# One substitution run for units 0 and 1, an unprepared unit 0, wider small matmuls and a new order in a deltanet and low-rank-mixer kernel

## The chip, the cores and the metric

The kernel runs on one core of a Trainium2 chip. A core has a matmul engine (PE, with its own weight loads, PEld), a vector engine (DVE), a scalar engine (ACT), a general engine (POOL), a queue engine (SP) and DMA queues. Each engine takes its instructions in the order in which they were written for it; semaphores hold an instruction back until what it reads is there. The metric is the device time of one execution in microseconds (us).

## The reference

Two blocks follow each other. The first is a delta-rule recurrence over 768 steps, for 4 batches x 8 heads of width 48; the second mixes tokens with a rank-32 product and then runs a two-layer channel MLP.

```python
k_n = k / (norm(k) + 1e-06)
for t in range(768):
    y[:, :, t] = q_t @ state                      # 48 x 48 state per head
    v_old = state^T k_t
    state = state + beta_t * outer(k_t, v_t - v_old)

x = y as (4, 768, 384)
u = x + ((x^T @ U) @ V)^T                         # U 768 x 32, V 32 x 768
out = u + relu(u @ w_ch1) @ w_ch2                 # 384 -> 1536 -> 384
```

## The kernel before

The recurrence is computed in chunks of 64 tokens. Within a chunk the steps form a unit lower triangular system, whose inverse (with beta and the norms in it) is called Z here. With it a chunk needs only matmuls: `z = Z v - (Z k) s`, `y = q s + (masked q k) z`, `s = s + k z`, where s is the state. Six chunks of all 8 heads of one batch make a unit; there are 8 units (2 for each batch, `units[n]`), which live in turn in two big tiles (`slots`). For a unit n the steps are:

- `load`: DMAs of k, q, v, and of `z` (a second copy of half of k with its token halves swapped, in `kz`), issued on SP, ACT and POOL.
- `grams`: PE transposes of k and q (`turn`, L672), copies by ACT (`placed`), then the products k k^T and q k^T (`products`, L700), of which DVE lays the 32-wide diagonal blocks into `diag` (L713) and masks the q k^T part (L731, one instruction for each half).
- `norms`: ACT root, then a chain of small DVE instructions to the scale `cp`, which is also copied onto the diagonal of `xt` (L627).
- `blocks`: DVE transposes the diagonal blocks into `gs` (L794), scales them (L798) and substitutes: for 31 columns, or 15 where a unit's 32-blocks are halved (units 0, 1 and 2), one product (L803) and one subtraction (L809) each. L816 transposes the result back into `zz`.
- `joins`: matmuls that put together 16-blocks into 32-blocks and these into 64-blocks. For units 0 and 1 (`lone`) the first two stages work on 64 x 64 tiles of the array with 16 moving columns (L860 and L874, 48 profile rows for each stage and half of a unit), the later ones on 32 x 32 tiles (L900 to L921).
- `prepare`: Z is multiplied into k (L1023) and v (L1034) for the whole unit, half by half.
- `recur` and `outputs`: for each chunk the matmuls on the state, L1072 (`b`), L1100 (the new state), L983 and L997 (the two parts of y), 16 rows each, with the DVE instructions L1085 (z) and L1111 (s) between them.

When all 12 chunks of a batch have their y in X, `front` does the token mixing (L1393, L1412, L1436) and `wide` the MLP in three blocks of 256 tokens (`channels` L1497, `narrow` L1617). The next batch's units run beside the MLP of the batch before. Ahead of the first `front` there is nothing of this kind: the head of the kernel holds units 0 and 1, all of batch 0's recurrence and, on ACT and DVE, the conversion of the 64-bit weights (`load_weights`: L1198 on ACT, L1212, L1219 and L1226 on DVE). Its raw data are staged in rooms of other tiles, two of them in w2_sb.

PSUM banks are handed out by the kernel in pairs. The order of everything is written out by hand: `ORDER` numbers some 2260 steps, and each engine receives its instructions in that order. So a step that waits holds all later steps of its engine.

The time lines below name the scalar engine's sequencer and the others' with a "q" (SPq). fp32 matmuls show as two rows each, transposes as one.

Of the kernel before, what the change touches and what calls it, by code (L numbers as in the profile page):

```python
# [27 lines left out]
def kernel(  # L28
# [114 lines left out]

    ORDER = """
    add_up b0 i0 f00: 590 628 635; add_up b0 i0 f03: 659 670 676; add_up b0 i1 f00: 795 820 825; add_up b0 i1 f03:
    840 846 849; add_up b0 i2 f00: 954 1014 1042; add_up b0 i2 f03: 1030 1053 1058; add_up b1 i0 f00: 1146 1147 1163;
    add_up b1 i0 f03: 1186 1188 1192; add_up b1 i1 f00: 1313 1315 1347; add_up b1 i1 f03: 1363 1364 1371; add_up b1
    i2 f00: 1482 1490 1493; add_up b1 i2 f03: 1543 1551 1561; add_up b2 i0 f00: 1688 1689 1692; add_up b2 i0 f03:
    1708 1721 1727; add_up b2 i1 f00: 1844 1845 1846; add_up b2 i1 f03: 1888 1889 1892; add_up b2 i2 f00: 2027 2051
    2056; add_up b2 i2 f03: 2046 2047 2053; add_up b3 i0 f00: 2183 2184 2189; add_up b3 i0 f03: 2187 2188 2190;  # L150
    add_up b3 i1 f00: 2205 2206 2208; add_up b3 i1 f03: 2203 2204 2207; add_up b3 i2 f00: 2226 2229 2230; add_up b3
    i2 f03: 2227 2228 2231; blocks n0: 67 71 72 73 76 78 79 80 84 85 88 95 100 101 102 106 107 109; blocks n1: 134
    151 155 160 162 169 192 196 200 208 209 212 220 222 226 232 233 235; blocks n2: 482 491 495 498 500 502 508 510
    511 513 516 519 521 522 528 529 530 537; blocks n3: 700 718 722 724 727 732 733 753 757 761 766 768 769 770 772
    774 778 784 787 791 792 798 799 811 812 814 815 819 824 831 847 848 851 854; blocks n4: 966 976 978 979 982 986
    988 997 1006 1020 1028 1029 1038 1048 1063 1072 1078 1082 1084 1094 1096 1106 1107 1108 1109 1111 1112 1113 1117
    1118 1121 1123 1125 1132; blocks n5: 1175 1190 1207 1210 1217 1219 1223 1224 1235 1236 1239 1246 1254 1258 1270
    1275 1279 1284 1285 1286 1290 1291 1294 1295 1298 1301 1302 1323 1324 1328 1331 1335 1336 1342; blocks n6: 1507
    1519 1531 1533 1542 1552 1559 1565 1570 1572 1574 1578 1579 1588 1591 1599 1606 1616 1628 1639 1640 1644 1645
    1649 1650 1654 1656 1660 1661 1663 1665 1667 1669 1677; blocks n7: 1670 1729 1732 1735 1742 1746 1754 1762 1768  # L160
    1776 1781 1782 1795 1797 1799 1805 1806 1810 1830 1832 1833 1835 1839 1847 1852 1857 1865 1868 1869 1871 1872
    1887 1890 1894; both f0: 2123; both f1: 2141; both f2: 2143; both f3: 2121; both f4: 2176; both f5: 2191;
    channels b0 i0 e0: 541 542; channels b0 i0 e1: 543 545; channels b0 i0 e2: 546 548; channels b0 i0 e3: 575 579;
    channels b0 i0 e4: 594 595; channels b0 i0 e5: 608 620; channels b0 i1 e0: 764 775; channels b0 i1 e1: 777 781;
    channels b0 i1 e2: 783 785; channels b0 i1 e3: 793 802; channels b0 i1 e4: 804 805; channels b0 i1 e5: 816 833;
    channels b0 i2 e0: 897 898; channels b0 i2 e1: 909 911; channels b0 i2 e2: 912 934; channels b0 i2 e3: 945 963;
    channels b0 i2 e4: 964 965; channels b0 i2 e5: 969 1002; channels b1 i0 e0: 1122 1137; channels b1 i0 e1: 1139
    1140; channels b1 i0 e2: 1141 1142; channels b1 i0 e3: 1145 1148; channels b1 i0 e4: 1149 1165; channels b1 i0
    e5: 1166 1167; channels b1 i1 e0: 1272 1304; channels b1 i1 e1: 1305 1307; channels b1 i1 e2: 1309 1310; channels
    b1 i1 e3: 1312 1314; channels b1 i1 e4: 1316 1333; channels b1 i1 e5: 1334 1350; channels b1 i2 e0: 1440 1441;  # L170
    channels b1 i2 e1: 1447 1449; channels b1 i2 e2: 1463 1464; channels b1 i2 e3: 1466 1499; channels b1 i2 e4: 1501
    1514; channels b1 i2 e5: 1515 1528; channels b2 i0 e0: 1668 1671; channels b2 i0 e1: 1672 1673; channels b2 i0
    e2: 1682 1684; channels b2 i0 e3: 1685 1686; channels b2 i0 e4: 1690 1699; channels b2 i0 e5: 1700 1701; channels
    b2 i1 e0: 1804 1808; channels b2 i1 e1: 1809 1812; channels b2 i1 e2: 1815 1827; channels b2 i1 e3: 1855 1858;
    channels b2 i1 e4: 1860 1861; channels b2 i1 e5: 1875 1877; channels b2 i2 e0: 1951 1961; channels b2 i2 e1: 1963
    1964; channels b2 i2 e2: 1966 1977; channels b2 i2 e3: 1984 1992; channels b2 i2 e4: 2002 2012; channels b2 i2
    e5: 2024 2034; copies f0: 2081 2091; copies f1: 2131 2135; copies f2: 2083 2092; copies f3: 2085 2109; copies f4:
    2155 2156; copies f5: 2149 2162; cut f0 k0 to0: 2116; cut f0 k0 to1: 2126; cut f0 k1 to1: 2114; cut f1 k0 to0:
    2144; cut f1 k0 to1: 2173; cut f1 k1 to1: 2178; cut f2 k0 to0: 2106; cut f2 k0 to1: 2172; cut f2 k1 to1: 2137;
    cut f3 k0 to0: 2134; cut f3 k0 to1: 2122; cut f3 k1 to1: 2138; cut f4 k0 to0: 2160; cut f4 k0 to1: 2177; cut f4  # L180
    k1 to1: 2193; cut f5 k0 to0: 2166; cut f5 k0 to1: 2192; cut f5 k1 to1: 2186; diagonals n0 h0: 189 190 191 213 214
    224; diagonals n0 h1: 167 168 172 178 181 194; diagonals n1 h0: 302 306 311 319 334 346; diagonals n1 h1: 286 297
    316 317 320 321; diagonals n2 h0: 572 573 574 588 593 611; diagonals n2 h1: 615 632 660 692 701 704; diagonals n3
    h0: 865 866 881 883 884 888; diagonals n3 h1: 858 859 860 861 869 900; diagonals n4 h0: 1161 1174 1203 1204 1213
    1216; diagonals n4 h1: 1155 1156 1157 1160 1195 1209; diagonals n5 h0: 1354 1362 1387 1392 1394 1396; diagonals
    n5 h1: 1359 1360 1365 1395 1405 1406; diagonals n6 h0: 1723 1726 1736 1758 1767 1772; diagonals n6 h1: 1710 1711
    1752 1785 1786 1792; diagonals n7 h0: 1900 1901 1903 1906 1909 1912; diagonals n7 h1: 1904 1910 1920 1927 1933
    1935; first f0: 2097; first f1: 2133; first f2: 2105; first f3: 2103; first f4: 2159; first f5: 2165; front b0
    i0: 487 496 504 505 526 535; front b0 i1: 556 567 607 625; front b0 i2: 626 639 662 671; front b1 i0: 1047 1057
    1066 1079 1101 1105; front b1 i1: 1225 1234 1241 1250; front b1 i2: 1344 1349 1404 1426; front b2 i0: 1576 1592  # L190
# [416 lines left out]

    def landed(name, n, j=1):
        return need(*[(name, n, g, j) for g in range(2)])

    def norms(n):

        _, _, _, _, _, vn, _, _ = units[n]
# [1082 lines left out]
```

## Time and profile before

| | us |
|---|---|
| median of 3 runs | 597.41 |
| lowest and highest run | 595.88, 597.56 |
| the profiled execution's own time | 596.68 |
| its span, first to last instruction | 595.0 |
| PE busy | 560.1 (94%) |
| DVE busy | 409.8 (69%) |
| ACT busy, POOL busy | 217.0, 133.3 |
| first matmul of unit 0's joins (L860) | at 32.0 |
| first matmul of the recurrence (L997) | at 57.7 |
| unit 1's `prepare` (L1034) begins | at 84.25 |
| last matmul of batch 0's recurrence ends | at 107.4 |
| first matmul of the MLP (L1497) | at 116.0 |

The profile's first part gives busy time by engine, the second the span in 40 slices of 14.9 us with busy tenths, the granted PE clock (PEclk, tenths of full speed) and DMA use. A group line reads "line engine operation out<-in shapes xcount | busy, mean ns | idle before". A line of a window table gives the stretch, its length, each engine's busy time with its number of rows, the granted clock, the DMA share and GB/s. Timeline rows give start, duration, engine, line and shapes. PE busy near 100% does not say that PE is at full speed: the clock row has to be read with it.

### The profile page before, as it was taken

To read this page: it belongs to the slowest core of one execution; us is meant where nothing else is said; L and a number is where in the kernel's file an instruction comes from. 1 tells how busy PE (TensorE), PEld (TensorE's weight loads), DVE (VectorE), ACT (ScalarE), POOL (GpSimd) and SP (SyncE) were. 2 spreads that over 40 slices of the span, in tenths; PEclk is the share of its full clock that TensorE was granted. 3 is DMA by queue.
4 is the path that set the end of the run, shared out by engine and by line. 5 is a ranking of instruction groups with operands and counts; after the bars stand their busy time and mean duration, and the time that the engine had idled before them with its cause. 6 is when DMAs were issued, how large, how long until landed. Compare 5 with 4: busy or idle time off the path is not lost.

```text
span 595.0 us, 23442 instructions
## 1 busy us (share of the span) xinstructions
PE 560.1 (94%) x10428; PEld 482.4 (81%) x10428; DVE 409.8 (69%) x1011; ACT 217.0 (36%) x442; POOL 133.3 (22%) x229
## 2 busy tenths in 40 slices
PE   4797987899999999999999999999999999999997
PEld 4696876688989987989889888898899778556997
DVE  3889767899999359999893389998973154122542
ACT  2558374436313442144234340234343321334000
POOL 8142133215041507312105143250110000000000
PEclk9657556999999999999999999999999999999999
DMA  9762656624041225510302035420201000000000
GB/s 141 152 154 72 216 116 146 140 70 70 3 95 22 46 42 91 99 47 17 75 2 41 11 54 93 105 58 15 68 6 37 3 2 15 26 0 1 26 28 28
DMA packets 89445, 36.23 MB, mean 61 GB/s; under 512 B 75456, under 2 KB 87104, under 8 KB 89344
## 3 DMA queue, kind: packets, MB, share of 16 engines
q1 hardware_dynamic: 80800, 24.69, 19.4%
q0 software_dynamic: 6944, 9.74, 8.2%
q8 instruction: 82, 1.34, 1.0%
q10 hardware_dynamic: 1600, 0.30, 0.3%
q14 instruction: 19, 0.16, 0.1%
HBM read 29.98 MB, written 4.72 MB: 58 GB/s over the span
## 4 chain that ended last, share of the span: by engine, by line
PE 90%; DVE 4%; issue 2%; ACT 2%; DMA 1%; SPq 0%; DVEq 0%; ACTq 0%
PE P L1617 29%; PE P L1497 25%; PE P L1296 7%; PE P L700 4%; PE P L1072 3%; PE P L983 2%; PE P L997 2%; PE P L672 2%; PE P L874 2%; PE P L1100 2%; PE P L1034 2%; PE P L1023 2%; PE P L860 2%; PE P L1412 2%; PE P L1436 1%
## 5 line engine op out<-in xcount | busy, mean ns | idle before, releaser
L1497 PE MATMUL P<-ut,w_sb 128*128 128x256 f32 x648 | 150.3, 385 | 0.9 <-ACT ut L1439 0.9
L1497 PEld LDWEIGHTS P<-ut,w_sb 128*128 128x128 f32 x648 | 119.8, 190 | 17.8 <-ACT ut L1439 1.1
L1617 PE MATMUL P<-w_sb,hs 128*128 128x192 f32 x540 | 95.8, 330 | 0.0
L1617 PEld LDWEIGHTS P<-w_sb,hs 128*128 128x128 f32 x540 | 87.4, 190 | 3.6 <-issue 1.8
L809 DVE TENSOR_TENSOR xt<-xt,prod 128x112 f32<-128x112 f32 (+21 forms) x200 | 64.6, 323 | 6.9
L803 DVE TENSOR_TENSOR prod<-gs,xt 128x112 f32<-128x112 f32 (+21 forms) x200 | 63.5, 318 | 3.6
L1537 DVE TENSOR_TENSOR X<-X,P 128x192 f32<-128x192 f32 x84 | 29.0, 348 | 49.6 <-PE P L1617 49.4
L1462 ACT ACTIVATE hs<-P 128x512 f32<-128x512 f32 x54 | 32.3, 598 | 80.0 <-PE P L1497 70.4
L967 ACT COPY X<-P 64x192 f32<-64x192 f32 x96 | 30.1, 313 | 60.7 <-PE P L997 59.6
L1617 PE MATMUL P<-w_sb,S 128*128 128x192 f32 x288 | 50.6, 330 | 0.0
L1617 PEld LDWEIGHTS P<-w_sb,S 128*128 128x128 f32 x288 | 46.6, 190 | 1.6 <-issue 1.2
L939 ACT COPY slot<-zz 32x384 f32<-32x384 f32 x64 | 32.2, 508 | 17.2 <-DVE zz L816 10.5
L555 POOL DMA_DIRECT2D slot<-in_v_dram x32 | 21.2, 665 | 66.9 <-DVE slot L747 33.4
L700 PE MATMUL P<-slot 48*64 48x64 f32 x1536 | 32.0, 235 | 4.4 <-ACT slot L687 3.7
L700 PEld LDWEIGHTS P<-slot 48*64 48x64 f32 x1536 | 28.9, 148 | 8.7 <-ACT slot L687 5.0
L1085 DVE TENSOR_TENSOR z<-slot,P 128x192 f32<-128x192 f32 x44 | 15.4, 350 | 29.2 <-PE P L1072 28.9
L946 POOL MEMSET slot<- 32x384 f32 x32 | 13.2, 413 | 96.0 <-PE P L900 52.2
L1296 PE MATMUL P<-slot,w_sb 128*128 128x384 f32 x96 | 33.2, 487 | 0.6 <-ACT slot L1365 0.6
L541 POOL DMA_DIRECT2D slot<-in_q_dram x40 | 24.6, 621 | 40.8 <-DVE slot L747 28.1
L541 POOL DMA_DIRECT2D slot<-in_k_dram x40 | 24.5, 620 | 35.5 <-DVE prod L803 18.6
L555 POOL DMA_DIRECT2D slot<-in_k_dram x44 | 29.5, 675 | 9.0 <-PE P L1100 8.7
L1305 DVE TENSOR_TENSOR slot<-slot,P 128x384 f32<-128x384 f32 x18 | 9.3, 551 | 32.4 <-PE P L1296 24.3
(153 smaller groups left out, 926.0 us busy)
## 6 DMA issues: line engine op xcount, KB each, us to landing
out_dram<-X SPq DMA_DIRECT2D x22, 192.0 KB, 2.6
w_sb<-in_moe_w_ch_dram SPq DMA_DIRECT2D x10, 384.0 KB, 5.2
slot<-in_k_dram SPq DMA_DIRECT2D x48, 72.0 KB, 3.4
slot<-in_k_dram POOLq DMA_DIRECT2D x44, 72.0 KB, 3.3
slot<-in_v_dram SPq DMA_DIRECT2D x32, 72.0 KB, 3.4
slot<-in_v_dram POOLq DMA_DIRECT2D x32, 72.0 KB, 3.6
X<-in_moe_w_ch_dram SPq DMA_DIRECT2D x6, 384.0 KB, 4.4
wide<-in_moe_w_ch_dram SPq DMA_DIRECT2D x6, 384.0 KB, 4.7
```

What stands on the lines that cost most here:

```text
L541: queue.dma_start(out=blocked(n)[quarter(y % 4), j, g, :, 0:w], in_=src[b, 4 * g + 2 * j + par, hf * UC * L : (hf + 1) * UC * L, BK * low ...
L555: queue.dma_start(out=t[half(1 - g if name == "z" else g), :, to, 0:D], in_=src[b, 4 * g + s, hf * UC * L : (hf + 1) * UC * L, :].rearrang ...
L700: nc.tensor.matmul(p_g[half(g ^ (par * i)), par, c], kq[rows, c, j, 0, half(g)], kq[rows, c, j, i, half(g)], start=True, stop=True,)
L803: nc.vector.tensor_tensor(out=prod, in0=gb[:, :, j : j + 1, j + 1 :].to_broadcast([128, split, m, w]), in1=xb[:, :, 0:m, j : j + 1].to_bro ...
L809: nc.vector.tensor_tensor(out=xb[:, :, 0:m, j + 1 :], in0=xb[:, :, 0:m, j + 1 :], in1=prod, op=ALU.subtract,)
L939: nc.scalar.copy(pg[quarter(i), :, at, :, a : a + BK], cut(zc, h)[quarter(i)].rearrange("p r (c j) t -> p r c j t", j=2),)
L967: nc.scalar.copy(x[half(c % 2), c // 2, 4 * D * g : 4 * D * (g + 1)].rearrange("p (j r d) -> p r j d", r=2, d=D), states(p_y)[half(g)],)
L1296: nc.tensor.matmul(to, w, t, start=start, stop=stop, skip_group_check=True)
L1462: nc.scalar.activation(hs[:, fs[0] : fs[1] + 1 : fs[1] - fs[0]], p_f, ACTF.Relu)
L1497: nc.tensor.matmul(p_f[:, x], w(x, t), ut[:, t], start=(t == 0), stop=(t == KT - 1))
L1537: nc.vector.tensor_tensor(out=to, in0=to, in1=p, op=ALU.add)
L1617: nc.tensor.matmul(to, of[0], of[1], start=of[2], stop=of[3], skip_group_check=True)
```

## The change

- Units 0 and 1 get their own `gs` and `xt` (`twins`), which lie in w2_sb where second-layer weights go later, so that one run of 15 column steps (4 groups in place of 2, `substitute`) does both units. `blocks(1)` then only transposes back. For unit 1 the result goes into the flat `gs` and `xt` (`inverses`). Unit 2 waits until unit 1 is joined, and the weights of w2 until both units are transposed back.
- The copy of the scale onto the diagonal of `xt` goes from DVE to ACT (`spread`); the two mask instructions for q k^T become one of 768 elements.
- The first two join stages of units 0 and 1 move 64 columns instead of 16: the same 16 columns are repeated four times (`REPEATS`), and only the first of the four results is read. The matmuls for y of batch 0 move 96 columns instead of 48 in the same way (`YREPEATS`).
- Nine `filler` steps on PE, each a 128 x 128 by 256 matmul of the identity into a free PSUM bank, read by nobody.
- Unit 0 has no `prepare` (`DIRECT`): each chunk does `v - k s` on DVE, then 8 matmuls with Z, then a copy by ACT to z.
- Units 0 and 1 keep their token halves in place (`NATURAL`), so their swapped copies of k are not loaded (8 DMAs less).
- A new `ORDER` of about 2240 steps.

```diff
+    FILLERS = (0, 1, 2, 3, 4, 5, 6, 7, 8)
+    early = w2_sb.rearrange("p m f d -> p (m f d)")
+    twins = [early[:, 2 * SIZE * y : 2 * SIZE * y + 2 * SIZE] for y in range(2)]
+    DIRECT = (0,)
+    NATURAL, ONCE = (0, 1), ()
+    REPEATS, YREPEATS = 4, 2
...
+        def substitute():
+            if twin:
+                xb, gb = (
+                    t.rearrange("p (u x) -> p u x", u=4)[:, :, 0 : size * BK].rearrange(
+                        "p u (a b) -> p u a b", b=BK
+                    )[:, :, :, 0:size]
+                    for t in twins[::-1]
+                )
+            us = 4 if twin else split
+            yield need(*[("c", x) for x in (range(NU) if twin else [n])], ("returned", n - 1))
+            for j in range(size - 1):
+                m, w = j + 1, size - 1 - j
+                prod = single.tile([128, us, m, w], FP32, name="prod", tag="prod")
...
-        yield need(("joined", n - 1))
+        if n != 1:
+            yield from substitute()
+        yield need(("substituted", 0) if n == 1 else ("joined", n - 1))
...
+                def moving(of):
+                    return of[:, None, :].to_broadcast([L, REPEATS, SB]) if lone else of
...
-                            p_e[rows, y], of, zc[rows, e, SB:BK], start=True, stop=True
+                            at(p_e, y)[rows], of, moving(zc[rows, e, SB:BK]), start=True, stop=True
...
+            if n in DIRECT:
+                emitted(("ready", n, h))
+                return
...
+            if direct:
+                for j, par, g in heads:
+                    nc.tensor.matmul(
+                        states(p_z)[half(g ^ par * (n not in NATURAL)), par, j],
+                        zt[half(g), par, cu, j],
+                        vn[half(g), cu, 2 * par + j],
+                        start=True,
+                        stop=True,
+                    )
+                z = zs[c] = small.tile([128, 4, D], FP32, name="z", bufs=3)
+                nc.scalar.copy(z.rearrange("p (r j) d -> p r (j d)", r=2), p_z)
...
-            yield need(("raised", i))
+            yield need(("raised", i), *[("returned", x) for x in range(NU)] * (i >= W2))
...
+    def filler(k):
+        nc.tensor.matmul(
+            one(x)[:, 0:256], ident, ident[:, None, :].to_broadcast([128, 2, 128]), start=True, stop=True
+        )
```

The new order on PE, in the steps that the prediction speaks of: unit 1's second k turn and its product come ahead of unit 0's second q turn and product; two fillers stand before the transposes of beta for the second unit, one among the last products, two within and two behind unit 0's join stages, where unit 1's first join stage comes in before unit 0's last ones; two more stand among the first chunks. On DVE the whole run of the substitution, with its scaling and the transposition back, has nothing between its instructions.

More of the change, by code (lines that the diff above doesn't have):

```diff
@@ L785, in seed @@
         def seed():
-            yield need(("returned", n - 1))
+            yield need(*[] if twin else [("returned", n - 1), *[("joined", 1)] * (n == NU)])
             yield op("pool", 1.05)
@@ L1655 @@
         begin(reserve(), 0)
+        for k in FILLERS:
+            begin(filler(k), 0)
         begin(weight_sums(), 97)
```

594 lines of the change are left out of this document (321 added, 273 removed).

## The prediction

> **What bounds the kernel now.** I read the page first: where is PE idle, and where is it not at full clock?
>
> ```profile
> span 595.0 us, 23442 instructions
> ...
> PE   4797987899999999999999999999999999999997
> ...
> DVE  3889767899999359999893389998973154122542
> ...
> PEclk9657556999999999999999999999999999999999
> ```
>
> From the ninth slice on PE is full and its clock whole: that part is PE's own work, 479 us of it. The first seven slices have clocks of 0.5 to 0.9, and DVE is often as full as PE. All the change's new instructions lie there. So second a table by stage, cut where the timeline shows unit 0's joins, the first chunk, unit 1's `prepare`, the last chunk and the first MLP matmul (columns: PE, PEld, DVE, ACT, POOL busy and rows, clock, DMA share, GB/s).
>
> ```profile
> 0.00:31.90 31.90, 19.53 (x384) 17.18 (x384) 20.80 (x68) 14.41 (x27) 14.98 (x31) 0.79 0.91 153
> 31.90:57.70 25.80, 22.15 (x721) 21.41 (x720) 22.84 (x63) 17.40 (x34) 9.40 (x15) 0.60 0.45 110
> 57.70:84.20 26.50, 23.16 (x736) 21.62 (x736) 19.19 (x36) 14.98 (x34) 2.78 (x6) 0.54 0.48 153
> 84.20:107.40 23.20, 17.39 (x621) 15.57 (x621) 16.46 (x31) 13.10 (x25) 9.30 (x16) 0.72 0.74 162
> 107.40:116.00 8.60, 6.90 (x146) 4.47 (x146) 7.71 (x23) 4.81 (x8) 3.26 (x5) 1.00 0.61 121
> 116.00:595.00 479.00, 470.95 (x7822) 402.15 (x7822) 322.76 (x794) 152.31 (x316) 93.62 (x157) 1.00 0.20 41
> ```
>
> I call these stages A to F. In B and C PE is busy 86 and 87% at half clock: they are PE's, and would be shorter at full clock. Third, PE alone in stretches of 3.41 us, since every change of clock lies a multiple of that from the others:
>
> ```profile
> 35.73:39.14 3.41, 3.41 (x68) 0.50 0.96 202
> 49.38:52.79 3.41, 3.41 (x114) 0.50 0.27 66
> 52.79:56.21 3.42, 2.23 (x145) 1.00 0.00 0
> ...
> 80.10:83.51 3.41, 3.27 (x116) 0.50 0.04 12
> 83.51:86.93 3.42, 3.14 (x120) 0.50 0.71 144
> 86.93:90.34 3.41, 1.68 (x104) 1.00 1.00 185
> ```
>
> Busy time doesn't set the next clock: the first stretch is busy throughout and stays at 0.5. What is moved does. I weigh each row's moved columns with its share of the array (a 64 x 64 tile is a quarter). The first stretch has 68 rows of 16 columns, 68 x 16 / 4 = 272. That at 49.38 has 48 + 48 rows of 64 and 18 of 48, about 1,560 by start times, and full clock follows; 83.51 has 1,520 and is followed by full clock; 80.10 has 1,408 and isn't; 86.93, at full clock, has 1,104 and loses it. Two stretches near 27 and 31 us, with transposes, had 1,540 to 1,560 and stayed at half. So some 1,500 a stretch is the border, give or take 100. Fourth, DVE's groups by shape, for the substitution:
>
> ```profile
> L803 DVE TENSOR_TENSOR prod<-gs,xt 128x252 f32<-128x252 f32 x10 | 4.1, 412 | 0.1
> ...
> L803 DVE TENSOR_TENSOR prod<-gs,xt 128x126 f32<-128x126 f32 x6 | 1.7, 290 | 0.2
> ```
>
> Double the elements cost 1.42 times as much.
>
> **The change, part by part.**
>
> *One substitution.* The 15 columns of one unit take 8.64 us (21.11 to 29.75). With four groups each step takes the row of twice the elements: L803 and L809 sum to 10.3 us, with the 0.035 us between instructions as now 11.4 us. Scaling takes 1.22 (the 1024 row) for 0.68. Two units: 12.6 in place of 18.6, so DVE saves 6.0. But unit 0 must wait for unit 1's scale. PE after the first beta transposes (18.04): turn 0.9, turn 1.47 (at half clock, as at 22.07), products 1.56 and 1.56, two fillers, beta 1.47. A filler is two rows of 256 columns; L1497's 36 such rows take 8.04 us, so 0.45 a filler, and 0.9 at half clock. That ends at 26.8. ACT 0.30, DVE 0.29 and the norms 1.0 give 28.4; the masks and the transposition of unit 1's blocks (1.95) fit before. Then 1.22 + 11.4 + 2.08 (L816): unit 0's joins start at **43.1 instead of 32.0**. Unit 1's result, returned at 55.9 now, comes by DVE's new order (masks, two L825, L816: 6 us) at 49. The copies moved to ACT (0.2) and the joined masks (0.95 for 1.1) gain 0.2 each on DVE; ACT's are beside DVE's scaling, else they cost 0.3.
>
> *Wider joins.* A stage of 48 rows takes 2.75 us at half clock (96 rows of L860 in 5.5) and 1.5 at full (47 rows from 56.08 in 1.53). With 64 columns the bounds are nothing, as weight loads of the same tiles cover it (products with 64 columns need 1.56 for 48 rows), and double, if columns and loads add up. I take nothing: the nearest row, L1023 with 64 x 64 tiles and 64 columns, is no slower for each row. A stage now weighs 768: 950 a stretch at half clock, 1,750 at full. So wider joins hold a full clock and don't raise a half one; a filler adds 512.
>
> *Stage B after.* At half clock: four stages of unit 0 11.0, four fillers 3.5, unit 1's first stage and a half 4.1, the small stages between 3: 21.5, and the first chunk at 64.7. `prepare` of unit 0, which follows the joins now (50.8 to 57.5), is gone. At full clock PE needs half, but DVE's list from 43.1 (10 instructions and the updates) lasts to 52.5, and what follows puts the first chunk at 57. Before: 57.7.
>
> *Unit 0 without `prepare`.* Each chunk gains 16 rows and an ACT copy on its chain: b, L1085, Z, ACT, L1100, L1111 are 0.43 + 0.35 + 0.43 + 0.31 + 0.41 + 0.35 and 0.3 of hops, 2.6 us at full clock, 3.2 at half. A chunk without Z takes 2.33 (90.41 to 92.74) at half clock, 1.75 at full by the same rows. Queued behind the added waits: on PE the join stages of unit 1, on ACT the copies of y.
>
> *Wide y.* 96 columns lie beyond the rows; from 27 ns a row at 48 and 32 at 64 columns 0.3 us more for 16 rows at half clock, 0.2 at full; between nothing (hidden while DVE makes z) and 0.3 x 23 = 7. Its weight goes from 192 to 384 a time. At full clock I take nothing on the chain.
>
> *Loads and POOL.* Eight DMAs of 72 KB less; they are issued between 12 and 38 us and nothing on the chain waits for them: nothing. POOL clears both units' `xt` ahead of 20 us (1.0 each, L788) instead of one at 32: nothing, as POOL's later steps are beside other work.
>
> *Weights of w2.* They wait for 49 us; L1219 for them comes after 90: nothing.
>
> *Stages C and D after.* C keeps six chunks, 2.5 stages of joins, two fillers: weight 10,900. If it ran at half clock for 28 us, that is 1,330 a stretch, in uneven lumps, and chunks without a gap reach 1,500. Once lifted, 20 us hold over 1,800. So I take C as mostly at full clock: 6 x (2.6 + 0.7, the share of other work) = 20. D starts with `prepare` of unit 1, which lifts the clock today too (83.51 above), and 1,152 a chunk with the turns of unit 2 then hold it. Its six chunks take 20.4 now, 3.4 each, 1.1 above the quickest; 6 x (1.75 + 1.1) + 1.7 until the first half is prepared (two lots of 48 rows) = 18.8. DVE must put some 46 us of work into the 58 of B to D, which it can. E loses one turn's place behind the products: 7.6.
>
> *Stage F.* The same PE steps but one product more (0.5), and 154 changes of form between big and small tiles for 146: 480.
>
> Sum: 43.1 + 21.5 + 20 + 18.8 + 7.6 + 480 = 591.0 span. The profiled execution is 1.7 longer than its span, and 0.7 under the median: **593 us**. Its own range, from C at 17 to 23, F at 478 to 482: 588 to 598.
>
> **A rule on the clock.** The row is 35.73: busy throughout, and half clock before and after. The Trainium skill, TensorE: Matmul & The Clock Gate (Part 1, What's actually happening), has the clock follow how busy PE is, and full after one busy window of about 3.4 us. By that rule widening and fillers buy nothing and the sum is rival 2's, by the row it is mine; this trace doesn't agree with the rule for small tiles.
>
> **The rivals.**
>
> 1. *Full clock already in the joins of B*, if the border for it lies lower than I read. Then B ends at 57: 57 + 20 + 18.8 + 7.6 + 480 + 2.4 = 586. For it: the fillers stand there. Against: 1,000 to 1,280 a stretch by my count.
> 2. *Busy time alone lifts the clock.* Stage B's joins fill a whole stretch, so the clock is full from 47 on: B ends at 58, and the time is 587. Against: 35.73.
> 3. *C stays at half clock* (the other side). Joins of 280 a us dilute the chunks, no stretch of C reaches 1,500, and the wider y and the fillers now cost: C is 28, D after its lift 20, sum 600.2 + 2.4 = **603**. It decides if C and D together last over 42.7 us (595 - 43.1 - 21.5 - 7.6 - 480), where they take 49.7 now and 38.8 in my sum. For it: the counts above lie just under the border.
> 4. *Stage F takes the gain back.* DVE is busy 4.9 of 5 us from 120 to 140, so what it hasn't done when the MLP starts early stalls PE: up to the 5 us won, 597. Against: DVE has 6 us less to do.
>
> **How the numbers follow.** My case 0.42, rival 1 0.17, rival 2 0.03, rival 3 0.26, rival 4 0.12. About 0.3%, 1.8 us, is what a measurement can tell from no change. Faster: 0.17 + 0.03 + most of 0.42 = 0.60. Same: half of rival 4, a little of my case and of rival 3, 0.11. Slower: 0.29. The range 584 to 604 leaves out the far halves of rivals 1 and 3.
>
> **What would show it.** Right: L816 of unit 0 ends near 43, the first chunk is near 65 at half clock, the clock is 1.0 for most of 70 to 95, unit 1's `prepare` comes near 85, the first L1497 counterpart at 111. Wrong: a join stage above 3 us at half clock (widening isn't free), a clock of 0.5 through C (rival 3), a clock of 1.0 from 47 (rivals 1 and 2), or PE gaps behind DVE in the first 40 us of the MLP (rival 4).

## The result and the profile after

The changed kernel is slower: 604.64 us median of 6 runs (603.90 to 605.38) against 597.48 us (595.88 to 599.36, 6 runs) for the kernel before, ratio 1.0114 with a 95% interval of 1.0087 to 1.0142. The profiled execution took 605.38 us, its span is 603.4. In the table of the experiments medians and ratios are of runs in the fast state; one run of `lean`, 612.87 us, was in the slow state and is left out. First the page of the changed kernel (line numbers are now those of the new file):

```profile
span 603.4 us, 23234 instructions
...
PE   4569887899999999999999998999999999999997
...
DVE  3895836999899668899875388989973134322532
...
PEclk9869968999999999999999999999999999999999
```

PE's clock is what the change was to lift, and it is lifted: the third to sixth slices, 5, 7, 5, 5 before, are 6, 9, 9, 6. Yet the full part of PE's row begins no earlier. The same table by stage as in the prediction, cut at the same events (first join, first chunk, unit 1's `prepare`, last recurrence matmul, first MLP matmul):

```profile
0.00:41.50 41.50, 21.97 (x486) 18.46 (x486) 28.55 (x76) 18.51 (x36) 18.45 (x36) 0.86 0.86 146
41.50:57.70 16.20, 14.88 (x416) 12.76 (x417) 12.35 (x21) 9.99 (x21) 2.56 (x5) 0.83 0.24 66
57.70:87.80 30.10, 25.44 (x816) 22.28 (x816) 17.47 (x31) 16.77 (x39) 1.96 (x4) 0.83 0.42 134
87.80:113.10 25.30, 20.05 (x683) 17.71 (x677) 17.67 (x29) 14.26 (x27) 12.19 (x19) 0.93 0.69 144
113.10:121.00 7.90, 6.13 (x100) 3.65 (x98) 7.23 (x25) 4.24 (x10) 1.04 (x2) 1.00 0.51 79
121.00:603.40 482.40, 473.80 (x7870) 403.32 (x7870) 323.31 (x777) 153.36 (x322) 94.70 (x160) 1.00 0.20 42
```

| stage | before | forecast | after |
|---|---|---|---|
| A, to unit 0's joins | 31.9 | 43.1 | 41.5 |
| B, to the first chunk | 25.8 | 21.5 | 16.2 |
| C, to unit 1's `prepare` | 26.5 | 20 | 30.1 |
| D, to the last recurrence matmul | 23.2 | 18.8 | 25.3 |
| E, to the MLP | 8.6 | 7.6 | 7.9 |
| F, the MLP part | 479.0 | 480 | 482.4 |

A and B together are 57.7 in both kernels: what one run of substitutions takes from B it adds to A. C and D, forecast 10.9 shorter, are 5.7 longer although their clocks rose from 0.54 and 0.72 to 0.83 and 0.93. PE's busy time in B to E, 69.6 us before, is 66.5: the higher clock took off 3.1. Busy time multiplied by clock estimates PE's work in full-clock microseconds. For B to E it was 22.15 x 0.60 + 23.16 x 0.54 + 17.39 x 0.72 + 6.90 = 45.2 before and is 14.88 x 0.83 + 25.44 x 0.83 + 20.05 x 0.93 + 6.13 = 58.2. So the clock gave little more than the added work took. The estimate is rough, since short rows do not shrink in full proportion: sixteen rows of L1072 took 0.72 us in C of before, at a clock of 0.54 (product 0.39), and 0.43 in F, at full clock. So part of the 13 us between the two sums comes from the measure and not from added work.

**Where that work lies in C.** PE's groups by shape between first chunk and unit 1's `prepare` (busy us, mean ns of one | idle before), first of the kernel before, then of the changed one:

```profile
L983 PE MATMUL P<-s,slot 48*64 48x48 f32 x80 | 3.7, 311 | 0.5 <-DVE s L1111 0.5
L1072 PE MATMUL P<-s,slot 48*64 48x48 f32 x80 | 3.6, 309 | 0.6 <-DVE s L1111 0.6
L997 PE MATMUL P<-z,slot 64*64 64x48 f32 x80 | 3.6, 305 | 0.1
```

```profile
L1070 PE MATMUL P<-z,slot 64*64 64x96 f32 x96 | 6.8, 292 | 2.2 <-issue 2.2
L1174 PE MATMUL P<-slot 64*64 64x48 f32 x96 | 5.2, 249 | 0.9 <-DVE slot L1164 0.5 <-issue 0.3
L1056 PE MATMUL P<-s,slot 48*64 48x96 f32 x80 | 3.7, 302 | 0.1
```

The wide y products (L1070, L1056) take as long at a clock of 0.83 as the narrow ones (L997, L983) at 0.54. L1174, the new product with Z, takes 5.2 for its 96 rows, 0.87 for each chunk where the prediction had 0.43 at full clock. By start and end times a chunk's sixteen rows take 0.62 at full clock and 1.09 at half, so both the clock and the rows themselves are in that mean. With `NATURAL` the rows' half is always the columns' half, so the matmuls of L1174 and L1070 lie on two positions of the array in turn, not four.

**The chain.** From the chain that ended last (start, duration, what), the piece of one chunk, from the state to the next state:

```profile
74.58 0.37 DVE s L1205
74.95 0.04 issue
74.99 0.45 PE P L1149 x16
75.44 0.49 PE P L1070 x10
75.93 2.16 issue
78.09 0.80 PE P L1070 x6
...
79.68 0.92 PE P L1174 x14
...
80.70 0.67 PE P L1056 x10
81.37 0.41 PE P L1194 x16
...
81.87 0.36 DVE s L1205
```

Between `b` (L1149) and Z (L1174) stand sixteen wide y products of an earlier chunk and small joins, and in their midst a gap of 2.16 us in which PE waited for no semaphore. From start and end times of each step, the waits above 0.25 us of the five chunks that follow the first:

```
chunk  period  waits: before what
1      5.64    s 2.67 (behind joins)
2      3.90    b 0.38, L1164 0.73
3      4.84    L1164 0.36, Z 0.27, s 0.91
4      7.28    Z 3.75 (2.16 of it the gap)
5      10.53   b 0.59, s 1.70, L1205 4.26
```

The periods sum to 32.2, the waits to 15.6; the rest is 3.3 a chunk. They end at 92.75: the last wait lies behind C's end, in D, and 11.4 of the waits before it. The longest is DVE's:

```profile
85.58 1.03 DVE L1320 SCALAR_TENSOR_TENSOR w_sb<-wide,w_sb 128x768 uint16<-128x768 uint32 x1
89.80 0.65 DVE L1306 TENSOR_SCALAR w_sb<-X 128x768 int32<-128x768 int32 x1 [3.19 <-ACT X L1292]
90.49 0.96 DVE L1313 SCALAR_TENSOR_TENSOR w_sb<-hs,w_sb 128x768 int32<-128x768 int32 x1
91.48 1.03 DVE L1320 SCALAR_TENSOR_TENSOR w_sb<-hs,w_sb 128x768 uint16<-128x768 uint32 x1
92.40 0.35 DVE L1205 TENSOR_TENSOR s<-s,P 128x192 f32<-128x192 f32 x1
```

The state (L1205) could start at 88.1, but ahead of it in DVE's queue stand three weight instructions, the first of which waits 3.19 us for ACT; ACT was behind the copies of the late y products.

**The clock.** PE in stretches of 3.41 us:

```profile
43.69:47.10 3.41, 3.41 (x46) 0.50 0.52 154
47.10:50.51 3.41, 3.41 (x119) 1.00 0.48 125
70.99:74.41 3.42, 2.82 (x129) 1.00 0.87 286
74.41:77.82 3.41, 0.97 (x30) 1.00 0.91 296
77.82:81.23 3.41, 3.14 (x90) 0.50 0.07 24
```

The stretch from 43.69, filled by 38 rows of widened joins and one filler, lifted the clock (in the prediction's measure 1,120 columns, not 1,500). It was lost in the stretch of the 2.16 us gap, at 77.82, for 10 us.

### The profile page after: what moved, and what is told of

The parts are those of the page before. It is cut to its first block, busy times and chain, and to the rows that moved or that the text cites. A ratio compares the mean times of both kernels' runs of the same rounds, so it can differ in the third digit from the quotient of the medians.

```text
span 603.4 us, 23234 instructions
## 1 busy us (share of the span) xinstructions
PE 562.3 (93%) x10350; PEld 478.2 (79%) x10350; DVE 406.6 (67%) x956; ACT 217.1 (36%) x452; POOL 130.9 (22%) x225
## 4 chain that ended last, share of the span: by engine, by line
PE 77%; DVE 15%; ACT 3%; issue 2%; DMA 1%; SPq 1%; DVEq 0%; ACTq 0%
PE P L1718 27%; PE P L1598 19%; PE P L1390 7%; DVE prod L837 3%; PE P L1070 3%; PE P L726 3%; PE P L1149 2%; DVE xt L843 2%; PE P L1194 2%; PE P L1110 2%; PE P L1056 2%; PE P L1099 1%; PE P L1506 1%; PE P L1530 1%; PE P L921 1%
## 5 line engine op out<-in xcount | busy, mean ns | idle before, releaser
L843 DVE TENSOR_TENSOR xt<-xt,prod 128x31 f32<-128x31 f32 (+20 forms) x170 | 57.0, 335 | 5.8
L837 DVE TENSOR_TENSOR prod<-gs,xt 128x31 f32<-128x31 f32 (+20 forms) x170 | 55.9, 329 | 3.2
L1563 ACT ACTIVATE hs<-P 128x512 f32<-128x512 f32 x54 | 32.0, 597 | 68.9 <-PE P L1598 64.7
L1164 DVE TENSOR_TENSOR z<-slot,P 128x192 f32<-128x192 f32 x39 | 13.6, 349 | 32.4 <-PE P L1149 32.3
L562 POOL DMA_DIRECT2D slot<-in_k_dram x40 | 24.5, 625 | 49.4 <-issue 21.1
L726 PEld LDWEIGHTS P<-slot 48*64 48x64 f32 x1536 | 27.1, 142 | 8.8 <-issue 5.1
L726 PE MATMUL P<-slot 48*64 48x64 f32 x1536 | 30.1, 228 | 4.0 <-issue 2.5
L1390 PE MATMUL P<-slot,w_sb 128*128 128x384 f32 x96 | 33.1, 486 | 0.0
L1004 ACT COPY slot<-zz 32x384 f32<-32x384 f32 x56 | 28.4, 508 | 11.5 <-DVE zz L861 8.4
L1070 PE MATMUL P<-z,slot 64*64 64x48 f32 (+1 forms) x720 | 27.7, 238 | 4.6 <-issue 3.0
L1718 PE MATMUL P<-w_sb,slot 128*128 128x192 f32 x180 | 30.5, 328 | 0.9 <-DVE X L1638 0.9
```

Of the source, the lines that this page charges most:

```text
L562: queue.dma_start(out=blocked(n)[quarter(y % 4), j, g, :, 0:w], in_=src[b, 4 * g + 2 * j + par, hf * UC * L : (hf + 1) * UC * L, BK * low ...
L726: nc.tensor.matmul(p_g[half(g ^ (par * i * (n not in NATURAL))), par, c], kq[rows, c, j, 0, half(g)], kq[rows, c, j, i, half(g)], start=Tr ...
L837: nc.vector.tensor_tensor(out=prod, in0=gb[:, :, j : j + 1, j + 1 :].to_broadcast([128, us, m, w]), in1=xb[:, :, 0:m, j : j + 1].to_broadc ...
L843: nc.vector.tensor_tensor(out=xb[:, :, 0:m, j + 1 :], in0=xb[:, :, 0:m, j + 1 :], in1=prod, op=ALU.subtract,)
L1004: nc.scalar.copy(pg[quarter(i), :, at, :, a : a + BK], cut(zc, h)[quarter(i)].rearrange("p r (c j) t -> p r c j t", j=2),)
L1070: nc.tensor.matmul(into(g, par, j), qk[at, par, cu, j], over(z[at, 2 * par + j]), start=(c == 0 and j == 0), stop=(j == 1), skip_group_che ...
```

## The experiments

Theory 1: the chain of the chunks in C and D was lengthened by waits in the queues of PE and DVE. Rival: PE's added work, which the clock does not outrun, fills C and D whatever the order. A third question is F, 3.4 longer: its order, its hand-over, or something else. In the table all ratios are to the kernel before on the same chip; "MLP" is the start of the first MLP matmul in the profiled execution.

| run | median us | ratio (95%) | first chunk | MLP | F |
|---|---|---|---|---|---|
| before | 597.48 | | 57.7 | 116.0 | 479.0 |
| changed | 604.64 | 1.0114 (1.0087 to 1.0142) | 57.7 | 121.0 | 482.4 |
| head_after | 610.27 | 1.0217 (1.0183 to 1.0251) | 57.2 | 118.4 | 490.0 |
| tail_after | 607.39 | 1.0163 (1.0122 to 1.0204) | 57.5 | 117.5 | 488.6 |
| w_late | 603.30 | 1.0105 (1.0072 to 1.0138) | 57.4 | 119.5 | 482.0 |
| swapped | 601.09 | 1.0072 (1.0050 to 1.0095) | 57.8 | 118.6 | 481.0 |
| before_wide | 595.36 | 0.9990 (0.9966 to 1.0013) | 56.7 | 114.2 | 480.1 |
| join_narrow | 615.75 | 1.0301 (1.0241 to 1.0361) | 64.2 | 131.2 | 482.7 |
| y_narrow | 603.16 | 1.0109 (1.0053 to 1.0164) | 57.2 | 120.4 | 481.9 |
| no_fill | 605.71 | 1.0154 (1.0115 to 1.0194) | 56.9 | 116.2 | 485.5 |
| y_late | 608.23 | 1.0156 (1.0114 to 1.0199) | 58.5 | 123.8 | 482.3 |
| combo | 601.53 | 1.0055 (1.0020 to 1.0091) | 57.6 | 118.7 | 482.3 |
| combo_late | 600.64 | 1.0041 (1.0011 to 1.0072) | 58.1 | 117.9 | 481.2 |
| prepared | 612.74 | 1.0257 (1.0212 to 1.0301) | 61.8 | 122.6 | 488.1 |
| lean | 604.89 | 1.0139 (1.0081 to 1.0198) | 57.8 | 115.8 | 482.9 |
| lean_y | 607.63 | 1.0169 (1.0132 to 1.0207) | 57.4 | 118.8 | 488.1 |

The medians come from different chips, on which the kernel before took 596.3 to 597.9, so versions are better compared by their ratios. The MLP column is of one execution each, and it varies: `head_after` has the changed kernel's steps up to the MLP and started it at 118.4, not 121.0, and `tail_after` has before's and started it at 117.5, not 116.0. Differences under 3 us in that column can't be told from chance. Stage C of the changed head was the same in both of its traces, 30.1 and 29.8.

**Head and tail exchanged.** Two orders were spliced at the first MLP step: the changed head with the order of before's tail, and the reverse. A step that is not ready where it is written lets the next ready one go first.

```diff
-ORDER: changed kernel, all steps
+ORDER (head_after): changed kernel up to `channels b0 i0 e0`, then the tail of before
+ORDER (tail_after): before up to `channels b0 i0 e0`, then the tail of the changed kernel
```

> The changed kernel up to the first MLP matmul, then the order of the kernel before. Theory: the 3.4 us that stage F gained (482.4 against 479.0) come from the new order of F itself (one product more, eight changes of form more): 604.6 - 3.4 = 601.2, with F at 479. Rival: F is longer because the new head hands over a DVE backlog and an unfinished unit 2: then F stays at 482 and the time at 604.6.

> The kernel before up to the first MLP matmul, then the new order. Theory (order of F alone): 597.5 + 3.4 = 600.9, with the first MLP matmul at 116 and F at 482. Rival (the hand-over): 597.5, F at 479.

Both expectations of each failed: 610.27 and 607.39, F of 490.0 and 488.6, where either order with its own head has 479.0 and 482.4. So neither forecast explains F's 3.4 us. In `tail_after` PE stands still for 12.5 us of F, against 8.6 in the changed kernel, 5.7 of them in gaps in which it waits for no semaphore, and two stretches run at half clock; both are taken up below. In `head_after` it stands still for 14.0, against 8.0 in the kernel before. Only one such gap is over 0.6 (0.82), but there are two waits of `b` for DVE's state, 2.4 together, in F's first 55 us, and one stretch at half clock behind the longer of them (1.86). So with this head a hand-over of late work is not excluded; the rest of its 11 us was not taken apart.

**The late weights.** Four `load_weights` steps that stand ahead of the state of chunk 5 (the weight instructions of DVE's lines above) are put behind it.

```diff
-350 load_weights; 353 load_weights; 355 load_weights; 356 load_weights; 357 recur b0
+357 recur b0; 358 load_weights; 359 load_weights; 360 load_weights; 361 load_weights
```

> The changed kernel with four weight steps of DVE moved from ahead of the state of chunk 5 to behind it. Theory: the chain of chunks waits in DVE's queue behind weight steps that wait for ACT; the L1205 of chunk 5 goes from 92.4 to about 88.3, the first MLP matmul from 121.0 to 117, the time to 600.6. Rival: PE's own queue (prepare of unit 1, wide y) holds the chain there anyway: L1205 earlier, but the first MLP matmul still at 120 to 121 and the time at 604.

603.30, nearer to the rival. The wait of 4.26 is gone (0.20), but `b` of the next chunk then waits 4.21 for PE, which is still at unit 1's `prepare`. By the ratios the gain is 0.5 us, which can't be told from nothing. A wait taken from one queue came back in another.

**The halves.** Units 0 and 1 get their swapped halves back, and with them eight loads.

```diff
-    NATURAL, ONCE = (0, 1), ()
+    NATURAL, ONCE = (), ()
-ORDER: ...
+ORDER: two steps "load n0 namez" and "load n1 namez" behind the last of each half's v
```

> The changed kernel with units 0 and 1 swapped again, as before (their second copies of k are loaded, 8 DMAs). Theory: keeping the halves in place puts L1070, L1174 and L1110 on two tile positions instead of four, which is why 16 rows of L1070 take 0.83 and 48 of L1110 1.49; swapped, they take about 0.55 and 0.9, and with some ten of them on the chain the time falls by 3 to 601.5. Rival: these steps lie beside the chain: 604.6, or above it if the eight loads delay k, q or v.

601.09, as the theory had it: 3.5 us less by the medians, 2.5 by the ratios, whose intervals just overlap, though eight loads more are issued. From the first chunk to the MLP it is 60.8, against 63.3 and, in `head_after`, 61.2. The rows show the cause more clearly than the times: L1067 and L1171, which were L1070 and L1174, between 57.7 and 87.8:

```profile
L1067 PE MATMUL P<-z,slot 64*64 64x96 f32 x96 | 5.3, 332 | 1.6 <-issue 1.6
L1171 PE MATMUL P<-slot 64*64 64x48 f32 x96 | 3.9, 267 | 1.3 <-issue 0.8 <-DVE slot L1161 0.5
```

They are busy 5.3 and 3.9 for 6.8 and 5.2, at a lower clock (0.72 for 0.83 in that stretch); sixteen rows of Z take 0.44 at full clock, for 0.62. Of the parts undone one at a time it brings the largest fall of the median.

**The widened joins**, once in the kernel before and once taken out of the changed one.

```diff
-                            p_e[rows, y], of, zc[rows, e, SB:BK], start=True, stop=True
+                            at(p_e, y)[rows], of, moving(zc[rows, e, SB:BK]), start=True, stop=True
...
-                        nc.tensor.matmul(p_d[rows, y], of, xe[rows, y], start=True, stop=True)
+                        nc.tensor.matmul(at(p_d, y)[rows], of, moving(xe[rows, y]), start=True, stop=True)
```

> The kernel before with one part of the change alone: the last products of the joins of units 0 and 1 have 64 columns instead of 16 (four copies of the same sixteen). In before's trace the stretch 35.73 to 39.14 us, filled by joins with 16 columns, leaves the clock at 0.5 until 52.79; in after's trace a stretch filled by joins with 64 columns (1,120 weighted columns) lifts it. Theory (the width decides the clock, and a full clock in the joins of unit 1 and the first prepare pays): the clock is 1.0 from about 39 to 43 us on, the first chunk starts 3 to 4 us earlier, time 593 to 594. Rival 1 (the head waits for the other engines, not for PE's clock): the clock rises as said, the time stays within 1.5 us of before. Rival 2 (widening doesn't lift the clock in before's order): the clock stays 0.5 to about 53 and the time is that of before.

```diff
-    REPEATS, YREPEATS = 4, 2
+    REPEATS, YREPEATS = 1, 2
```

> The changed kernel with the joins' last products back at 16 columns, all else as it is. Theory (the widened joins are what lifts the clock at 47 us, and that brought the first chunk to 57.7 us instead of the 64.7 forecast): the clock stays at 0.5 until about 60 us, the first chunk starts 3 to 6 us later than 57.7, time 607 to 610. Rival (the chain of the other engines holds the joins and chunks anyway): 604 to 605.5, with the first chunk within 1.5 us of 57.7.

Without the width the changed kernel takes 615.75: its clock is 0.5 from 39.9 to 80.9 and the first chunk comes at 64.2. So in the changed kernel the width is worth 11 us, more than the theory had. In the kernel before it holds the clock too, and yet 595.36 against 596.5 is no difference that this comparison can tell from none, as the first rival had it. Stage B of that run and, below it, of the run with narrow joins:

```profile
32.70:57.10 24.40, 17.59 (x730) 16.17 (x734) 22.98 (x64) 17.61 (x35) 9.33 (x15) 0.86 0.39 105
```

```profile
42.70:64.20 21.50, 21.46 (x418) 18.55 (x418) 12.16 (x21) 10.48 (x22) 2.25 (x5) 0.50 0.17 50
```

In before's order PE needs 17.59 for 22.15, but DVE is busy 22.98 of 24.40: B was DVE's, at 22.84 of 25.8 already before. In the changed order DVE has 12 us to do in B and PE fills it to 21.46 of 21.50. (The clock of the first run was up at 30.92, a stretch ahead of the joins, so it shows that wide joins hold the clock, not that they lift it; the second shows that without them it isn't lifted, though the fillers are there.)

**Wide y and fillers**, each taken out alone.

```diff
-    REPEATS, YREPEATS = 4, 2
+    REPEATS, YREPEATS = 4, 1
```

> The changed kernel with the y products of sequence 0 back at 16 columns, all else as it is. Theory (the wide y products stand ahead of the chunks' products on PE and cost more than the clock they hold): 0.3 to 0.4 us less for each of some eight groups that stand ahead of a chunk, first MLP product 2 to 3 us earlier, time 601 to 603. Rival (they are what keeps the clock at 1.0 from 57 to 78 us): the clock falls to 0.5 by 62 to 68 us and the time is 606 to 609.

```diff
-    FILLERS = (0, 1, 2, 3, 4, 5, 6, 7, 8)
+    FILLERS = ()
```

> The changed kernel without its nine filler products on PE during the substitution. Theory (the clock had fallen at 26.6 us with them and falls again at 40.27, before the joins begin at 41.5, so they bring nothing and stand in nobody's way): time within 1.5 us of 604.6, joins from 41 to 42 us on. Rival 1 (they hold the clock for the joins): joins at half clock two stretches longer, first chunk 2 to 4 us later, time 607 to 609. Rival 2 (they delay products of unit 1 on PE): time 601 to 603.

Narrow y is 48 columns for 96 (the 16 in two of the expectations is the number of rows in a group). It gives 603.16, not to be told from 604.64: the products are shorter, and the clock falls 5 us earlier (72.6 for 77.8). In both traces it falls about a long gap of PE without a semaphore, 2.68 here and 2.16 there, so the fall can't be put down to the width. Without fillers the clock is again 0.5 when the joins begin and rises at 47, as the theory had it, but in that execution it then stayed at 1.0 from 74 on, past the start of the MLP at 116.2, 4.8 earlier (2.2 earlier than in `head_after`). F then took 485.5, so most of the head's gain was lost there, and the median, 605.71, is not told from 604.64.

**Order or work.** In `y_late` the y products and joins that stand between a chunk's own products go behind its s (the lines show part of the moved steps). In `combo` swapped halves, narrow y and late weights are joined; `combo_late` adds the order of `y_late` to it.

```diff
-244 joins n0 h1; 246 joins n0 h1; 247 joins n1 h0; 250 joins n1 h0; ...; 259 recur b0
+recur b0 (s of chunk 1); joins n0 h1; joins n0 h1; joins n1 h0; joins n1 h0
-267, 276 outputs; 279 recur b0; 287, 288 outputs; 292, 296, 298 joins n1; 303 recur b0
+recur b0 (s of chunk 2); outputs; outputs; recur b0 (s of chunk 3); outputs; outputs; joins n1
-306 outputs; 308, 310 joins n1; 317 outputs; 319 recur b0; 334, 337 outputs; 344 recur b0
+recur b0 (s of chunk 4); outputs; joins n1; outputs; recur b0 (s of chunk 5); outputs; outputs
```

> The changed kernel with the order of the first chunks alone changed: the y products of chunks 1 to 5 and the joins' products that stand on PE between a chunk's own products (b, Z, s) are moved behind the s product of that chunk. In the changed kernel's trace s of chunk 1 waits 2.67 us behind joins, s of chunk 3 0.91, Z of chunk 4 3.75 (2.16 of it PE's own gap), s of chunk 5 1.70. Theory (order: the chunks stand in the wrong place of PE's queue): unit 1's prepare starts 3 to 5 us before 87.8 and the time is 600 to 602. Rival (work: between the first chunk and unit 1's prepare PE is busy 25.4 of 30.1 us, and what is moved still stands ahead of the prepare): prepare within 1.5 us of 87.8, time 603.5 to 606.

> The changed kernel with three parts undone together: halves swapped for units 0 and 1 (Z, K-side and prepare products on four tile positions again, eight loads back), y products 16 columns wide, and four load_weights steps behind chunk 5's s. Alone they gave 601.1 (from 604.6), 603.2 and 603.3. Theory (each takes work or a wait off the path between first chunk and first MLP product, and they add): 598 to 600. Rival (each only uncovers the next one's wait): no better than the halves alone, 600.5 to 602.

> The three undone parts of the run with swapped halves, narrow y and late weights, and also the order in which y and join products stand behind each chunk's s. If PE's work decides the head, this gives that run's time within 1 us; if the order does, 3 to 5 us less, 594 to 597, as fast as the kernel before or faster.

`y_late`: s of chunk 1 waits 0.49 for 2.67 and Z of chunk 4 0.12 for 3.75, but unit 1's `prepare` starts at 88.5 (87.8). The same work stood elsewhere, as the rival said. The time rose to 608.23; y came later to ACT, and the wait of L1205 grew from 4.26 to 7.79. `combo` and `combo_late`, in which the weight steps of that wait stand behind the state, differ by 0.9 us with overlapping intervals: this order is not the limit. That fits PE's work as the limit, but it is one order of many. And the three parts of `combo` do not add: 601.53 is the halves alone.

**Z multiplied ahead.** Unit 0 is prepared again.

```diff
-    DIRECT = (0,)
+    DIRECT = ()
-ORDER: 12 of the steps "recur b0" (Z and its copy, six chunks)
+ORDER: "prepare n0 h0" and "prepare n0 h1", four steps each, behind the joins
```

> The changed kernel with unit 0 prepared as before: K and V are multiplied by Z ahead of its chunks (eight PE steps and their ACT copies, behind its joins), and the Z product and its copy leave the chain of the six chunks. Theory (the multiplication in the recurrence is what lengthened the chunks, six times Z 0.65, copy 0.33 and their waits, 6 to 8 us, while the prepare delays the first chunk by 3 to 5): first chunk at 61 to 63 us, unit 1's prepare at 83 to 86, time 600 to 602.5. Rival 1 (PE's work decides, and the prepare is more of it than six Z products): time 605 to 609. Rival 2 (they weigh the same): within 1.5 us of 604.6.

612.74, worse than all three forecasts. Its MLP starts at 122.6, 1.6 and 4.2 behind the two traces of the changed head, so the multiplication in the recurrence is a small gain at most; the rest is F at 488.1.

**Without the added work.** `lean` has swapped halves, narrow y, late weights and no fillers; `lean_y` has the wide y. They keep the single run, Z in the recurrence and the widened joins.

```diff
-    FILLERS = (0, 1, 2, 3, 4, 5, 6, 7, 8)
+    FILLERS = ()
-    NATURAL, ONCE = (0, 1), ()
-    REPEATS, YREPEATS = 4, 2
+    NATURAL, ONCE = (), ()
+    REPEATS, YREPEATS = 4, 1
```

> The changed kernel with what adds PE work taken out except the widened joins: no fillers, narrow y products, halves swapped for units 0 and 1, and the four late weight steps. In the traces PE's busy time ahead of the first MLP product, weighted with the granted clock, is 59.8 us before and 78.9 after the change (fillers 5.6 of it, y and K-side outputs 7.3, prepare, Z and their like 4.7 more than before), while the busy time by the clock on the wall is 91.6 and 92.2. Theory (the work that was to hold the clock used up what the clock gave): weighted work falls to 61 to 64, the first MLP product comes at 114 to 117, time 596 to 599, level with before. Rival (the first chunk comes no earlier than before, 57.7, since one run of substitutions starts only when unit 1's scales are there, and the rest is the chain of six plus six chunks): first MLP product at 118 to 119, time 600.5 to 602.

> The same with the wide y products left in. Against the run with narrow y this tells what the wide y products cost or hold by themselves once the fillers and the halves are gone. Theory (work that pays for itself at best): within 1.5 us of the narrow one. Rival (they hold the clock between 57 and 85 us): clock 1.0 there and 2 to 4 us faster than the narrow one.

Stages B to E of `lean`:

```profile
42.10:57.80 15.70, 12.80 (x409) 12.29 (x410) 12.15 (x21) 10.02 (x21) 3.87 (x7) 0.81 0.34 87
57.80:84.60 26.80, 21.51 (x818) 18.89 (x815) 16.24 (x31) 16.74 (x40) 1.60 (x5) 0.70 0.46 150
84.60:108.00 23.40, 19.23 (x674) 17.00 (x674) 17.58 (x30) 14.45 (x28) 12.97 (x19) 0.76 0.74 154
108.00:115.80 7.80, 5.41 (x94) 3.08 (x93) 7.29 (x25) 4.10 (x9) 1.77 (x3) 1.00 0.54 86
```

The work is 12.80 x 0.81 + 21.51 x 0.70 + 19.23 x 0.76 + 5.41 = 45.5, before's 45.2, and the MLP starts at 115.8, where before's starts. So in this trace the theory holds for the head: fillers, wide y and two-position products cost at least what their clock gave, and what is left, the single run, Z in the recurrence and wide joins, brings the MLP no earlier. But the median, 604.89, is not level, and by the ratios not told from the changed kernel; this trace was the fastest of its executions. `lean_y` is not told from `lean` either; its clock was 1.0 only from 61.3 to 75.0 and then 0.5 to 88.7, so the rival failed. Two more traces of the same kernel were taken to see where the others lose:

> The kernel without fillers, wide y and two-position products once more, for a second trace of it: its first trace was the fastest of five executions (600.4, the others up to 608.8 at lower mean clocks), with the first MLP product at 115.8. If the head decides the spread, an execution of 605 to 609 has its first MLP product at 121 to 124; if the tail does, the first MLP product is at 115 to 117 and the tail holds stretches of half clock behind gaps of PE, some 488 us of it.

> The same kernel and the same two expectations, a third trace.

They took 608.51 and 608.29, with the MLP from 118.6 and 116.7 and F of 488.2 and 489.9. The loss is mostly F's. What F shows there, in `lean_c` (timeline of PE, and the two stretches around it):

```profile
344.11 1.65 PE L722 MATMUL P<-slot 48*64 48x64 f32 x94
347.72 0.37 PE L722 MATMUL P<-slot 48*64 48x64 f32 x2 [1.96 <-issue]
```

```profile
344.20:347.62 3.42, 1.56 (x102) 1.00 0.73 151
347.62:351.03 3.41, 3.31 (x9) 0.50 0.14 30
```

After 94 short matmuls PE stands still for 1.96 us with no semaphore to wait for; the stretch is busy 1.56 of 3.42, and the next, full of MLP matmuls, runs at half clock. `lean` has one such gap in F (1.31, at 201) and one stretch at half clock, `lean_b` two gaps (1.59, 1.96) and two stretches, `lean_c` two (1.84, 1.96) and three. The changed kernel has one gap, 1.31, which the border between two stretches divides, and keeps its clock; before has one of 0.66. `tail_after` has three, 2.04, 1.40 and 2.29, with two half-clock stretches, `prepared` three with two, `no_fill` two with one. The third stretch of `lean_c` lies behind no such gap.

## Why the prediction was wrong

The span came out 12.4 over the sum (603.4 for 591.0): A and B together 6.9 under it, C and D 16.6 over, E 0.3 and F 2.4 over.

- *B and C are PE's and would be shorter at full clock.* Right in part. In `before_wide` B's clock rose from 0.60 to 0.86 and C's from 0.54 to 0.66, and they took 24.4 for 25.8 and 24.9 for 26.5: in B DVE was as full as PE.
- *Stage A, 43.1.* It came at 41.5. The substitutions took 11.5 for 11.4, the scaling 1.22 as worked out. Right.
- *Wider joins cost nothing.* Right: 48 rows took 2.83 at half clock (2.75 in the sum) and 1.5 at full.
- *The border of 1,500 columns, joins that hold a full clock and don't raise a half one.* Wrong: the stretch 43.69 raised it, and the first chunk came at 57.7, not 64.7. That is the course of rivals 1 and 2 up to there, and by itself it made the head faster than forecast. Of the rule in rival 2 (the Trainium skill, TensorE: Matmul & The Clock Gate, Part 1, What's actually happening: one busy window lifts the clock) this stretch is an instance; the stretch 35.73 of before, just as busy with 16 columns, remains one against it. In `join_narrow` eleven stretches in a row, 43.36 to 80.91, are busy throughout, and only the last is followed by full clock. Weighted columns don't decide alone either: 1,024 in `no_fill` (43.6 to 47.0) lifted the clock, 1,104 in `join_narrow` (70.67 to 74.08) and 1,408 in before (80.10) didn't. What the clock follows stays open.
- *Stage C, 6 x (2.6 + 0.7) = 20, and D, 6 x (1.75 + 1.1) + 1.7 = 18.8.* This is the step that failed, and it decided the sign. The chain without waits was 3.3 a chunk for 2.6, and the share of other work, put at 0.7, was 3.1: 15.6 us of waits over the five chunks from 60.6 to 92.75, which reach 5 us into D. The sum priced a chain at full clock and gave other work the remainder. But C holds 25.44 us of PE work at a clock of 0.83, which alone is 21.1 at full clock, more than the 20 of the whole stage. Its terms: Z was priced at 0.43 and took 0.62 at full clock and 1.09 at half, since the two tile positions of `NATURAL` were not seen (0.44 at full clock in `swapped`, and 2.5 us of the time by the ratios); DVE's weight steps that wait for ACT were not looked for (4.26, though undoing it moved the wait to PE and gained no measurable time); PE's gap of 2.16 and the half clock after it were not foreseen. In D the five chunks after 92.75 took 17.45 us, 3.5 each for 2.85; their waits were not taken apart, so for D the cause is open in part.
- *Wide y costs nothing on the chain at full clock.* By time right, as far as can be told (`y_narrow` and `lean` against `lean_y` show no difference), but it didn't hold the clock either.
- *E, 7.6.* 7.9, right.
- *F, 480.* 482.4. Busy and idle time together, the products of k and q take 1.7 us more than before (48 more rows, and a gap of 1.31 for 0.66), the y products 1.3 more and L1390 1.7 less than its counterpart L1296; where the rest of the 3.4 lies is open. Rival 4's stall isn't there: no gap of PE behind DVE in F is over 0.65.
- *Rival 3* named the condition that came true (C and D over 42.7, or 42.8 by its own terms: they last 55.4) and a time, 603, near the result, but not the cause: it had C at half clock, which C was not.
- *The whole gain.* The sum counted DVE's 6 us and unit 0's `prepare` as won; A + B, 57.7 twice, shows that DVE's part only moved, and `lean` shows the head without the added work level with before's (MLP at 115.8, 118.6 and 116.7 in three traces, 116.0 and 117.5 in two of before's head).

No version tried is faster than before by a measurable amount; the widened joins alone (595.36 against 596.5) come nearest.

## What to carry to other kernels

Before you pay for PE's clock with extra columns, estimate busy time times clock for the stage with and without them, and look for the engine that is second: the same wide joins were worth 11 us in an order where PE filled the stage and nothing that could be measured where DVE did. A stage is bounded from below by the sum of an engine's work, not only by its chain; price both and take the longer. When halves or layouts are changed, count the tile positions that a group of small matmuls uses.

## What the runs showed of the hardware

PE's gaps without a semaphore go with packets of the queue that the profile calls "instruction". In 18 traces of these kernels there are 83 such gaps above 0.6 us after 32 us; each ends 1.2 to 1.9 us (median 1.43) after a 16 KB packet of that queue has landed. The changed kernel has 81 of these packets for 20,700 rows of matmuls and weight loads, the kernel before 82 for 20,856: about one packet for every 255 rows of PE. In the changed kernel such a packet lands at 76.60 and PE goes on at 78.09; in `lean_c` at 346.46 and 347.72. The gaps come behind dense runs of short matmuls: 94 in 1.65 us above, and 82 or more in the 4 us before every one of them (median 134). That PE outruns its instructions there is the reading that fits; it was not tried by an experiment. What a gap costs is more than itself: a stretch with 1.45 (`no_fill`), 1.56 (`lean_c`) or 2.10 us (`lean`) of busy time lost the clock for the next 3.4 us. The changed kernel kept it, as its gap at 370.8 left 2.55 and 2.66 of two stretches:

```profile
367.95:371.36 3.41, 2.55 (x151) 1.00 0.59 113
371.36:374.78 3.42, 2.66 (x35) 1.00 0.49 65
```

Busy time alone doesn't tell which: over these traces the stretches that lost the clock were busy for up to 2.58 us (one 3.11), while some with 1.85 to 2.1 kept it. And the same kernel falls into them or not from one execution to the next: three traces of `lean` have F at 482.9, 488.2 and 489.9. Why a given execution falls into one stays open.
